# Moving a scan, four left-out steps and the last stores in a TensorE-bound recurrence + MLP kernel

One core of a Trainium2 chip. The metric is the device time of one execution in microseconds; the median of several is given. A "span" is the time from the first to the last instruction in one profiled execution; it is 1.7 to 2.1 us shorter than the time.

## The reference

```python
sig = 1 / (1 + exp(-f_logit))                        # x, f_logit: (4, 6080, 256)
f = lower_bound + (1 - lower_bound) * sig
for t in range(S):                                   # recurrence along the sequence
    h = f[:, t] * h + (1 - f[:, t]) * x[:, t];  y[:, t] = h
h = y.reshape(24320, 256) @ w_in                     # w_in: (256, 2048)
out = (h * cos(h)) @ w_out                           # w_out: (2048, 256), float32 out
```

## The kernel before

The 24,320 tokens are cut into 7 chunks of 256 and 44 of 512. For each chunk ScalarE and GpSimd make the gate `ih` and the input term `u`, the DMA transposes them to `it` and `ut` (for chunks 0 to 3 TensorE does), GpSimd makes the forget factor `ff`, VectorE scans, GpSimd casts the result to `yb`. Then TensorE multiplies by `w_in` (mm1), ScalarE takes the cosine, VectorE the product T, and TensorE multiplies T by `w_out` (moe2). Steps are written (chunk, group). In the traces each engine's instructions come in the program's order (VectorE's scan, T, scan, T of the changed kernel start at 34.60, 35.48, 36.60 and 37.26).

```python
HALVED = (NSMALL, NSMALL + 1, NSMALL + 2)     # NSMALL = 7: 512-token chunks done as two 256s
pa[c, g] = ppool.tile([P, 2 * CH // n, n], f32, tag="p1", bufs=3, ...)   # mm1's output, 3 buffers
# ... cut
def moe2(c, h):
    # ... cut: half of a 128-token tile, 8 matmuls
    if last:
        nc.vector.tensor_copy(osb[:, ts, :], ps[:, ts % 2, :])
        nc.sync.dma_start(out[t0 + ts * P:t0 + (ts + 1) * P, :], osb[:, ts, :])
# ... cut: weaving of the next chunks' gates and scans into the steps
    if c == NPE:                                            # NPE = 4, the fifth chunk
        f, slots = (c - 2, 3), ((c - 2, 3), (c - 2, 3))     # where forget and the two scans go
    elif c <= NSMALL:
        f, slots = (c - 2, 0), ((c - 2, 3), (c - 1, 0))
    else:
        f, slots = (c - 1, 0), ((c - 1, 2), (c - 1, 4))
    at(*f, later(forget, c))
    for i, slot in enumerate(slots):
        at(*slot, later(recur, c, i), later(cast, c, i))
    # ... cut
    at(*second, later(less_one, c), later(pool_term, c), later(turn, c))
at(2, 2, later(emit_load, NSMALL))
SKIP = ((NSMALL, 5), (NSMALL + 1, 3), (NSMALL + 2, 1), (NSMALL + 2, 7))
steps = [(c, h) for c in range(1, NC) for h in range(2 * chunks[c][1] // P)]
for s in range(2, NC):
    if s > 2 and s + 5 < NC:
        emit_load(s + 5)
    for g in range(groups(s)):
        moe1(s, g)                                          # mm1, cosine, product
        if (s, g) not in SKIP:
            moe2(*steps.pop(0))
        for what in weave.get((s, g), []):
            what()
for c, h in steps:
    moe2(c, h)
```

A full-size chunk needs all its T before its second half-step; a small or halved one needs half of them. So moe2 must fall four steps further behind while the kernel passes from small to full chunks: that is what the four left-out steps (SKIP) do. They are made up at the end.

Of the kernel before, what the change touches and what calls it, by code (L numbers as in the profile page):

```python
# [17 lines left out]
def kernel(  # L18
        ctx: ExitStack, tc: tile.TileContext, x: bass.AP, f_logit: bass.AP,
        lower_bound: bass.AP, w_in: bass.AP, w_out: bass.AP, out: bass.AP):  # L20
    nc = tc.nc
# [3 lines left out]
    P = 128  # L25
# [9 lines left out]
    NSMALL = 7  # L35
# [6 lines left out]
    t0 = 0  # L42
# [25 lines left out]
    def hold(what, c, shape, dtype, bufs):  # L68
        if (what, c) not in held:
            held[what, c] = wpool.tile(shape, dtype, tag=what, bufs=bufs,  # L70
                                       name=f"{what}{c}")
        return held[what, c]
# [172 lines left out]
    def groups(c):  # L245
        return NJ * chunks[c][1] // (2 * CH)

    HALVED = (NSMALL, NSMALL + 1, NSMALL + 2)

    def room(c, g):  # L250
        if (c, g) not in pa:
            n = HALF if c in HALVED else chunks[c][1]
            pa[c, g] = ppool.tile([P, 2 * CH // n, n], f32, tag="p1", bufs=3,
# [3 lines left out]
    def mm1(c, g, a=0, b=None):  # L257
        n = chunks[c][1]
        first = 0
        if c in HALVED:  # L260
            n = HALF
# [15 lines left out]
    def cosine(c, g):  # L277
        n = HALF if c in HALVED else chunks[c][1]
        cs[c, g] = wpool.tile([P, 2 * CH // n, n], f32, tag="cs", bufs=3, name=f"cs{c}_{g}")
        nc.scalar.activation(cs[c, g], pa[c, g], AFT.Sin, bias=float(_HALF_PI), scale=1.0)  # L280

    def product(c, g):
        n = HALF if c in HALVED else chunks[c][1]
        jg = 2 * CH // n
        T = wpool.tile([P, jg, n], f16, tag="T", bufs=24, name=f"T{c}_{g}")
        nc.vector.tensor_tensor(T, pa[c, g], cs[c, g], AOP.mult)  # L286
        for jq in range(jg):
            if c in HALVED:
                for ts in (g // 4 * 2, g // 4 * 2 + 1):
                    Tt[c, ts, jg * (g % 4) + jq] = T[:, jq, ts % 2 * P:(ts % 2 + 1) * P]  # L290
            else:
                for ts in range(n // P):
                    Tt[c, ts, jg * g + jq] = T[:, jq, ts * P:(ts + 1) * P]

    def moe1(c, g):
        mm1(c, g)
        cosine(c, g)
        product(c, g)
# [3 lines left out]
    def moe2(c, h):  # L302
        t0, n = chunks[c]
        nt = n // P
        ts, half = h // 2, h % 2
        last = c == NC - 1
        if half == 0 and (ts % 2 == 0 or last):
            p2[c] = ppool.tile([P, 2, D], f32, tag="p2", bufs=2, name=f"pb{c}_{ts}")
        osb = hold("osb", c, [P, CH // P, D], f32, 2)
        ps = p2[c]  # L310
        for jt in range(half * NJ // 2, (half + 1) * NJ // 2):
            nc.tensor.matmul(ps[:, ts % 2, :], Tt[c, ts, jt],  # L312
                             wo[:, jt, :], start=(jt == 0), stop=(jt == NJ - 1))
        if half == 0:
            return
        if last:
            nc.vector.tensor_copy(osb[:, ts, :], ps[:, ts % 2, :])  # L317
            nc.sync.dma_start(out[t0 + ts * P:t0 + (ts + 1) * P, :], osb[:, ts, :])
        elif ts % 2 == 1:
            nc.scalar.copy(osb[:, ts - 1:ts + 1, :], ps)  # L320
            if ts == nt - 1:
                nc.sync.dma_start(
                    out[t0:t0 + n, :].rearrange("(k p) d -> p k d", p=P),
                    osb[:, 0:nt, :])
# [73 lines left out]
    moe1(0, 3)  # L398
    moe1(1, 0)
    moe2(0, 0)  # L400
    gate(2)
    term(2)
# [5 lines left out]
    settle(2)  # L408
    product(1, 2)
    moe2(0, 1)  # L410
    moe1(1, 3)
    moe2(0, 2)
    moe2(0, 3)
    gate(3)
# [7 lines left out]
    def at(s, g, *what):  # L422
        weave.setdefault((s, g), []).extend(what)

    def later(f, *args):
        return lambda: f(*args)

    for c in range(3, NC):
        if c < NPE:
            at(c - 1, 1, later(turn, c), later(forget, c), later(gate, c + 2),  # L430
               later(settle, c))
            continue
        if c == NPE:
            f, slots = (c - 2, 3), ((c - 2, 3), (c - 2, 3))
        elif c <= NSMALL:
            f, slots = (c - 2, 0), ((c - 2, 3), (c - 1, 0))
        else:
# [4 lines that stand above are left out]
        first, second = FRONT.get(c, ((c - 3, groups(c - 3) - 1), (c - 2, 0)))  # L442
        if c != NPE + 1:
            at(*first, later(gate, c))
        at(*second, later(less_one, c), later(pool_term, c), later(turn, c))

    at(2, 2, later(emit_load, NSMALL))
    SKIP = ((NSMALL, 5), (NSMALL + 1, 3), (NSMALL + 2, 1), (NSMALL + 2, 7))
    steps = [(c, h) for c in range(1, NC) for h in range(2 * chunks[c][1] // P)]
    for s in range(2, NC):  # L450
        if s > 2 and s + 5 < NC:
            emit_load(s + 5)
        for g in range(groups(s)):
            moe1(s, g)
            if (s, g) not in SKIP:
                moe2(*steps.pop(0))
# [34 lines left out]
```

## Time and profile before

| | before |
|---|---|
| time, median of 3 | 681.11 us (680.96 to 682.25) |
| span of the profiled execution | 679.7 us |
| TensorE / VectorE / ScalarE / GpSimd busy | 99 / 86 / 76 / 46% |
| granted TensorE clock | 1.000 |

In the timeline each line is a run of like instructions: start, length, engine, line, operation, count and, in brackets, the idle time before it and what ended it. For TensorE compare starts, not lengths (eight matmuls from 35.06 are 1.04 long, and the next eight start 0.87 on). The prediction shows the lines that carry the argument.

### The profile page before, as it was taken

Reading aid. Unit: us, or ns where it says so; the run is one execution under the profiler, and the core shown is the slowest. Engines: PE = TensorE matmul, PEld = TensorE weight load, DVE = VectorE, ACT = ScalarE, POOL = GpSimd, SP = SyncE. Lnnn points to the kernel's source line nnn. Section 1 sums busy time; section 2 is a strip of 40 time slices with the busy share of each in tenths; the row PEclk is TensorE's granted clock in tenths of the full one; section 3 lists DMA queues with packets and bytes.
Section 4 is the critical chain, followed back from the end, with each engine's and each line's share of the span. In section 5 each row is a group of like instructions: output and inputs, shape, how many; then the busy total and the mean of one; then the engine's idle time right before and its main releaser. Section 6 shows DMA issues by size and latency. Waiting matters only on the chain.

```text
span 679.7 us, 12405 instructions
## 1 busy us (share of the span) xinstructions
PE 670.9 (99%) x4826; PEld 494.6 (73%) x4826; DVE 583.2 (86%) x507; ACT 518.2 (76%) x587; POOL 315.1 (46%) x442
## 2 busy tenths in 40 slices
PE   7999999999999999999999999999999999999998
PEld 4899987777777777777777777777777777777776
DVE  5898998888888888888888888888888888888884
ACT  6887788777877788777877788777877788777762
POOL 5478454445454445445454445445454445445300
DMA  8799756656667556764776556764686566632301
GB/s 205 198 259 225 201 157 154 169 140 124 160 188 150 124 140 175 167 139 125 159 189 150 124 142 175 158 148 124 163 185 149 124 144 178 162 76 63 94 32 62
DMA packets 173290, 101.99 MB, mean 150 GB/s; under 512 B 99120, under 2 KB 172080, under 8 KB 173232
## 3 DMA queue, kind: packets, MB, share of 16 engines
q1 hardware_dynamic: 171680, 99.11, 59.5%
q0 software_dynamic: 1280, 2.10, 1.7%
q8 instruction: 37, 0.61, 0.4%
q14 instruction: 21, 0.17, 0.1%
q10 hardware_dynamic: 272, 0.00, 0.0%
HBM read 54.00 MB, written 24.90 MB: 116 GB/s over the span
## 4 chain that ended last, share of the span: by engine, by line
PE 88%; DVE 4%; DMA 3%; issue 2%; ACT 1%; POOL 1%; SPq 0%; ACTq 0%; DVEq 0%; POOLq 0%
PE pb L312 45%; PE pa L271 43%; DVE T L286 3%; DVE ya L218 2%; DMA wo<-in_moe_w_out_dram 1%; DMA wir<-in_moe_w_in_dram 1%; ACT cs L280 1%; DMA zt<-in_f_logit_dram 1%; ACT ig L122 0%; SPq L82 0%; POOL wo L106 0%; POOL u L163 0%; ACT ig L150 0%; POOL xt L82 0%; POOL zt L82 0%
## 5 line engine op out<-in xcount | busy, mean ns | idle before, releaser
L286 DVE TENSOR_TENSOR T<-pa,cs 128x1024 f16<-128x1024 f32 x380 | 449.1, 1212 | 81.5 <-ACT cs L280 81.1
L280 ACT ACTIVATE cs<-pa 128x1024 f32<-128x1024 f32 x380 | 389.3, 1028 | 144.0 <-PE pa L271 132.4
L312 PE MATMUL pb<-wo,T 128*128 128x256 f16 x3040 | 393.0, 273 | 0.6 <-DMA wo<-in_moe_w_out_dram 0.6
L271 PE MATMUL pa<-yb,wi 128*128 128x512 f16 (+2 forms) x1736 | 390.3, 353 | 2.9 <-DMA wi<-in_moe_w_in_dram 1.4
L312 PEld LDWEIGHTS <-T 128*128 128x128 f16 x3040 | 297.3, 98 | 100.1 <-issue 1.0
L271 PEld LDWEIGHTS <-wi 128*128 128x128 f16 x1736 | 193.3, 114 | 75.5 <-issue 2.0
L232 POOL TENSOR_SCALAR yb<-ya,hc 128x512 f16<-128x512 f32 (+1 forms) x97 | 65.8, 679 | 187.5 <-DVE ya L218 186.6
L218 DVE TENSOR_TENSOR_SCAN ya<-ff,ya,ut 128x512 f32<-128x512 f32 (+4 forms) x94 | 131.3, 1398 | 0.6 <-POOL ff L199 0.6
L163 POOL TENSOR_TENSOR u<-ig,xt 128x256 f16<-128x256 f32 x182 | 130.3, 748 | 0.0
L161 POOL CAST ih<-ig 128x1024 f16<-128x1024 f32 (+1 forms) x47 | 47.5, 1010 | 137.1 <-ACT ig L150 135.1
L199 POOL TENSOR_SCALAR ff<-it,hp 128x512 f32<-128x512 f16 (+1 forms) x94 | 62.9, 683 | 1.5 <-DMA it<-ih 1.5
L320 ACT COPY osb<-pb 128x512 f32<-128x512 f32 x93 | 53.8, 579 | 0.7 <-PE pb L312 0.7
L122 ACT ACTIVATE ig<-zt 128x1024 f32<-128x1024 f32 (+2 forms) x52 | 51.7, 994 | 2.0 <-DMA zt<-in_f_logit_dram 1.9
L150 ACT ACTIVATE ig<-ig 128x1024 f32<-128x1024 f32 x44 | 46.9, 1066 | 0.0
L339 PE MATMUL warm<-junk 128*128 128x512 f16 x15 | 5.7, 543 | 1.3 <-POOL junk L328 1.3
L218 DVE TENSOR_TENSOR_SCAN ya<-ff,ya,tp 128x256 f32<-128x256 f32 (+1 forms) x8 | 5.0, 665 | 1.3 <-ACT ff L196 1.3
L218 DVE TENSOR_TENSOR_SCAN ya<-ff,ut 128x320 f32<-128x320 f32 (+2 forms) x6 | 5.6, 928 | 0.0
L317 DVE COPY osb<-pb 128x256 f32<-128x256 f32 x4 | 1.7, 424 | 4.5 <-PE pb L312 4.5
L139 DVE SCALAR_TENSOR_TENSOR u<-ig,xt 128x512 f16<-128x512 f32 (+1 forms) x5 | 3.2, 645 | 2.5 <-DMA xt<-in_x_dram 1.7
L339 PEld LDWEIGHTS <-junk 128*128 128x128 f16 x18 | 2.1, 126 | 4.0 <-issue 2.2
L137 POOL TENSOR_SCALAR ih<-ig 128x512 f16<-128x512 f32 x2 | 1.7, 866 | 6.2 <-ACT ig L122 6.2
L99 POOL CAST wi<-wir 128x512 f16<-128x512 f32 x2 | 1.5, 748 | 4.9 <-DMA wir<-in_moe_w_in_dram 4.8
(29 smaller groups left out, 27.2 us busy)
## 6 DMA issues: line engine op xcount, KB each, us to landing
zt<-in_f_logit_dram SPq DMA_DIRECT2D x44, 512.0 KB, 5.1
xt<-in_x_dram SPq DMA_DIRECT2D x44, 512.0 KB, 6.0
out_dram<-osb SPq DMA_DIRECT2D x43, 512.0 KB, 3.4
out_dram<-osb SPq DMA_DIRECT2D x7, 256.0 KB, 5.1
zt<-in_f_logit_dram SPq DMA_DIRECT2D x5, 256.0 KB, 5.2
xt<-in_x_dram SPq DMA_DIRECT2D x5, 256.0 KB, 5.6
wir<-in_moe_w_in_dram SPq DMA_DIRECT2D x2, 512.0 KB, 5.4
wo<-in_moe_w_out_dram POOLq DMA_DIRECT2D x4, 256.0 KB, 7.1
```

Source lines behind the costliest of these rows:

```text
L122: nc.scalar.activation(ig[:, ks, :], zt[:, ks, :], AFT.Tanh, bias=0.0, scale=0.5)
L150: nc.scalar.activation(ig[:, ks, :], ig[:, ks, :], AFT.Identity, bias=-1.0, scale=1.0)
L161: nc.gpsimd.tensor_copy(by_half(ih), split(ig))
L163: nc.gpsimd.tensor_tensor(by_half(u)[:, k], split(ig)[:, k], split(xt)[:, k], AOP.mult)
L199: nc.gpsimd.tensor_scalar(f[:, a:b], igt[:, i, 0:b - a], hp[:, i:i + 1], 1.0, AOP.mult, AOP.add)
L218: nc.vector.tensor_tensor_scan(ya[:, p:q], f[:, p:q], ut[:, i, p - a:q - a], init, AOP.mult, AOP.add)
L232: nc.gpsimd.tensor_scalar(yb[:, a:b], held[f"ya{i}", c][:, a:b], hc[:, i:i + 1], 0.0, AOP.mult, AOP.add)
L271: nc.tensor.matmul(pa[c, g][:, jq, a:b], win_block(i, jt), held[f"yb{i}", c][:, first + a:first + b], start=(i == 0), stop=(i == ND - 1))
L280: nc.scalar.activation(cs[c, g], pa[c, g], AFT.Sin, bias=float(_HALF_PI), scale=1.0)
L286: nc.vector.tensor_tensor(T, pa[c, g], cs[c, g], AOP.mult)
L312: nc.tensor.matmul(ps[:, ts % 2, :], Tt[c, ts, jt], wo[:, jt, :], start=(jt == 0), stop=(jt == NJ - 1))
L320: nc.scalar.copy(osb[:, ts - 1:ts + 1, :], ps)
```

## The change

The intent: put the fifth chunk's second scan behind a product, so that TensorE gets its buffer back in time; place the left-out steps where VectorE has no scan; and let two engines share the last copies and stores.

```diff
-    HALVED = (NSMALL, NSMALL + 1, NSMALL + 2)
+    HALVED = tuple(range(NSMALL, NSMALL + 4))
...
         if last:
-            nc.vector.tensor_copy(osb[:, ts, :], ps[:, ts % 2, :])
-            nc.sync.dma_start(out[t0 + ts * P:t0 + (ts + 1) * P, :], osb[:, ts, :])
+            for i, (copy, queue) in enumerate(((nc.vector.tensor_copy, nc.sync),
+                                               (nc.scalar.copy, nc.scalar))):
+                ds = slice(i * P, (i + 1) * P)
+                copy(osb[:, ts, ds], ps[:, ts % 2, ds])
+                queue.dma_start(out[t0 + ts * P:t0 + (ts + 1) * P, ds], osb[:, ts, ds])
...
         if c == NPE:
-            f, slots = (c - 2, 3), ((c - 2, 3), (c - 2, 3))
+            f, slots = (c - 2, 3), ((c - 2, 3), (c - 1, 0))
...
-    SKIP = ((NSMALL, 5), (NSMALL + 1, 3), (NSMALL + 2, 1), (NSMALL + 2, 7))
+    SKIP = tuple((c, 6) for c in HALVED)
```

Part 1 is the scans, part 2 the halved chunks with their left-out steps, part 3 the end.

## The prediction

> **What bounds the kernel now.** I read the page first (busy shares), then the groups with shapes kept apart, then the timeline of TensorE, and only where TensorE waits those of VectorE, GpSimd and ScalarE. The groups' columns are: count | busy us, mean ns | idle before.
>
> ```profile
> PE 670.9 (99%) x4826; PEld 494.6 (73%) x4826; DVE 583.2 (86%) x507; ACT 518.2 (76%) x587; POOL 315.1 (46%) x442
> ...
> L286 DVE TENSOR_TENSOR T<-pa,cs 128x1024 f16<-128x1024 f32 x380 | 449.1, 1212 | 81.5 <-ACT cs L280 81.1
> L312 PE MATMUL pb<-wo,T 128*128 128x256 f16 x3040 | 393.0, 273 | 0.6 <-DMA wo<-in_moe_w_out_dram 0.6
> ```
>
> TensorE is 99% busy, but 273 ns is the length of a pipelined matmul, not its pace. The pace is the distance of starts in its timeline:
>
> ```profile
> 35.06 1.04 PE L271 MATMUL pa<-yb,wi 128*128 128x256 f16 x8
> 35.94 1.04 PE L312 MATMUL pb<-wo,T 128*128 128x256 f16 x8
> 37.45 1.03 PE L271 MATMUL pa<-yb,wi 128*128 128x256 f16 x8 [0.47 <-DVE T L286]
> 38.32 1.04 PE L312 MATMUL pb<-wo,T 128*128 128x256 f16 x8
> ...
> 60.15 1.23 PE L271 MATMUL pa<-yb,wi 128*128 128x256 f16 x8
> 61.22 1.04 PE L312 MATMUL pb<-wo,T 128*128 128x256 f16 x8
> ...
> 82.18 1.04 PE L312 MATMUL pb<-wo,T 128*128 128x256 f16 x8
> 83.22 1.03 PE L271 MATMUL pa<-yb,wi 128*128 128x256 f16 x8
> ...
> 98.06 1.04 PE L271 MATMUL pa<-yb,wi 128*128 128x256 f16 x8
> 99.45 1.05 PE L271 MATMUL pa<-yb,wi 128*128 128x512 f16 x4 [0.35 <-DVE T L286]
> ```
>
> Eight 256-column matmuls take 0.873 us from start to start (35.06 to 35.94). One step is a first-product group (L271) plus half a second-product tile (L312), 1.745 us. From 21.5 to 668 us every start follows at this pace except four: 37.45 should be 36.81 (0.64 late), the group of 60.15 stretches by 0.20, 83.22 should be 83.05 (0.17), 99.45 should be 98.93 (0.52). So 1.53 us, 0.2% of the span, is all that any reordering between 21.5 and 668 us can win. After 99.45 all is even.
>
> [...]0.873/8 = 109.1 ns, and four of 512 columns take about 0.864 us. Halving a chunk thus costs some 8 ns a group.
> [...]the four u products (L163) take 2.80 us clear of scans and 4.66 across two scans (54.40 below).
> [...]
> [...]Here the last 128 KB stores land a median of 1.7 us after issue[...].
>
> **Part 1, the fifth chunk's scans in two slots.** The gap at 37.45 waits for a PSUM buffer of three: T of step (3,0) stands on VectorE behind both scans of chunk 4, which themselves waited for GpSimd.
>
> ```profile
> 34.67 1.60 DVE L218 TENSOR_TENSOR_SCAN ya<-ff,ya,ut 128x256 f32<-128x256 f32 x2 [0.61 <-POOL ff L199]
> 36.20 4.61 DVE L286 TENSOR_TENSOR T<-pa,cs 128x1024 f16<-128x1024 f32 x4
> ```
>
> The program order of the changed kernel is scan, T(3,0), scan, T(3,1). Scan 34.67 to 35.5, T to about 36.65, scan to 37.35, T(3,1) to 38.5. The buffer is free at 36.65, before 36.81; the next is wanted at 38.55, so 0.05 to spare. The gap goes: 0.64 us won there. But is it kept? The second scan is 0.85 later, and so are all GpSimd's items behind its cast, down to the transpose (it) for chunk 6, issued at 39.23 now and about 40.1 then. That costs nothing: loads issued from 35.49 fill the queue, and in the packet records the transpose's 256-byte packets start only at 43.6. GpSimd then runs without a pause until TensorE's next stall:
>
> ```profile
> 45.73 0.94 POOL L199 TENSOR_SCALAR ff<-it,hp 128x256 f32<-128x256 f16 x2 [1.27 <-DMA it<-ih]
> 46.62 1.04 POOL L161 CAST ih<-ig 128x1024 f16<-128x1024 f32 x1
> 47.62 3.58 POOL L163 TENSOR_TENSOR u<-ig,xt 128x256 f16<-128x256 f32 x4
> ...
> 54.40 4.66 POOL L163 TENSOR_TENSOR u<-ig,xt 128x256 f16<-128x256 f32 x4
> 59.04 1.36 POOL L232 TENSOR_SCALAR yb<-ya,hc 128x512 f16<-128x512 f32 x2
> ```
>
> The second yb of chunk 7 is done at 60.40; TensorE's group of 60.15 ran two matmuls and waited for it. With part 1 TensorE comes to it at 59.51 but finds the chain started by the same landing (45.7) and of the same length (14.67 us). The group goes on at 60.4 as before. **Part 1 nets 0.0**, at most 0.1 if the scans, now earlier, overlap less with u.
>
> **Part 2, four halved chunks, skips at step 6 of each.** Before, four second-product steps were left out at (7,5), (8,3), (9,1), (9,7); now at (7,6), (8,6), (9,6), (10,6). The work is the same (four left out, done at the end); the halved chunk 10 costs 8 groups x 8 ns = 0.07 us. A step with a skip takes TensorE 0.873 us where VectorE's T alone takes 1.21, so it spends the lead of the buffers; scans stand in steps 2 and 4. From 60.4 on, by hand:
> (7,7) and (8,0) fall at 71.7 and 73.44 as now. (8,6) moves to 83.92, and T(8,3), ending at 83.18, no longer holds it: 0.17 won. (9,0) comes at 86.54, T(8,5) ends about 86.56 plus 0.04 for the semaphore: 0.06 lost anew. (10,0) comes at 99.68, T(9,5) ends about 99.65: 0.01 lost. With (10,0) at 99.69 and one skip of 0.873 still to come, this equals 98.82 against 99.45 now, plus 0.07 for the halving: **part 2 wins 0.56 us**. (11,0) comes at 112.8, T(10,5) about 112.7: no new loss, if barely. The second product keeps its operands: its tightest step now is (7,5), at 69.95, whose T(7,3) ends 69.85 and is used only by its second half.
>
> **Part 3, the last tiles in halves.** The end now (count, then duration ns min/median/max):
>
> ```profile
> 676.43 0.42 DVE L317 COPY osb<-pb 128x256 f32<-128x256 f32 x1 [1.32 <-PE pb L312]
> ...
> L318 SPq DMA_DIRECT2D out_dram<-osb x4: 332/338/345, 671.6 to 676.9; - x4
> ```
>
> Copy to 676.86, store issued 676.89, landed 678.58, span end 679.68. The intent is two copies side by side. But in the built program's order with waits, each of ScalarE's last four copies waits for VectorE, not TensorE: [...]they run one after the other. VectorE's half: 424 ns less 128 columns at 1.04 ns = 0.29, to 676.72. ScalarE's half: 579 ns at 512 columns less 384 at 0.83 = 0.26, plus 0.03 for the wait, to 677.03. The last store is issued at 677.06 instead of 676.89: 0.17 later. Half the bytes save perhaps 0.1. Then the final SyncE sequence checks eight queue semaphores one by one, 0.06 us each: the last landing is now the sixth, with three behind it (678.60 to 678.78); in the changed program it is the first, with seven behind, 0.25 later. **Part 3 loses about 0.3 us.**
>
> Sum: 0.0 - 0.56 + 0.3 = -0.25. From 681.11 that is 680.9.
>
> **Rivals.**
> (a) Part 1's 0.64 survives, because the chain on GpSimd starts earlier or is shorter. For: u takes 4.66 against 2.80, so 1.9 us is contention that moves with the scans. Against: the packets' queue and the unbroken chain. It would make 680.2 to 680.3.
> (b) A new wait: the 0.05 and 0.03 us of room at (4,0), (9,0), (10,0) and (11,0) are as small as my reading errors. If each step-6 skip stalls by 0.2 to 0.4 on T of step 5, part 2 wins nothing: 681.4 to 682.
> (c) The end is helped after all: a 64 KB store lands much faster, as two issues side by side. For: less data per queue.[...] It would make 680.5.
> (d) VectorE becomes the bound. Against: per full chunk it has 8 x 1.21 + 2 x 1.49 = 12.7 us of work in 13.9, and 13.1 in a chunk with a skip, still above.
>
> **Range and chances.** All the winnable stalls and the end together are under 2 us of 681, so 2% (13.6 us) is out of reach both ways. (a) and (c) together reach 679.9; (b) with the end's loss reaches 682. The spread of the three runs before is 1.3 us, upward. So 679.8 to 682.0. Faster by over 2% 0.01, within 2% 0.98, slower 0.01.
>
> **What would show it.** Right: no gap near 37; the first group of chunk 7 broken, resuming at 60.3 to 60.5 after yb; no stall over 0.1 us from 62 to 115; the first full-size group of chunk 11 near 112.8; ScalarE's last copy starting after VectorE's ends; from the last matmul to the span's end about 3.6 us instead of 3.3. Wrong: chunk 7 starting near 59.6 (rival a), stalls on T behind step 6 (b), an end shorter than 3.3 us (c).

## The result

The changed kernel takes 681.80 us (median of 6, 681.31 to 682.95), the kernel before 681.26 on the same occasions (6 runs). The ratio is 1.0009, with a 95% interval of 0.9996 to 1.0022: the same, and no gain to be seen. Ratios here are the mean of one kernel's fast runs over that of the other's of the same rounds, so not quite the ratio of the medians. The profiled span went from 679.7 to 679.9.

First the chain that ended last, by engine, from the page of the kernel before and then of the changed one.

```profile
PE 88%; DVE 4%; DMA 3%; issue 2%; ACT 1%; POOL 1%; SPq 0%; ACTq 0%; DVEq 0%; POOLq 0%
```

```profile
PE 91%; DMA 4%; POOL 3%; issue 1%; DVE 1%; SPq 0%; ACT 0%; POOLq 0%; DVEq 0%
```

VectorE's share of that chain went from 4 to 1% and GpSimd's from 1 to 3: it now runs through GpSimd where it ran through VectorE. (The shares count the work on the chain, not the waits.) TensorE's timeline of the changed kernel shows what it waits for:

```profile
35.90 1.04 PE L312 MATMUL pb<-wo,T 128*128 128x256 f16 x8
36.77 1.04 PE L271 MATMUL pa<-yb,wi 128*128 128x256 f16 x8
...
58.65 1.04 PE L312 MATMUL pb<-wo,T 128*128 128x256 f16 x8
60.17 0.27 PE L271 MATMUL pa<-yb,wi 128*128 128x256 f16 x1 [0.48 <-POOL yb L232]
60.84 0.93 PE L271 MATMUL pa<-yb,wi 128*128 128x256 f16 x7 [0.40 <-POOL yb L232]
...
86.05 1.04 PE L312 MATMUL pb<-wo,T 128*128 128x256 f16 x8
87.07 1.06 PE L271 MATMUL pa<-yb,wi 128*128 128x256 f16 x8
...
113.30 1.03 PE L271 MATMUL pa<-yb,wi 128*128 128x512 f16 x4
```

The gap near 37 is gone. In its place chunk 7's first group waits for both its `yb`: due at 59.53 (58.65 + 0.873), it starts at 60.17 (0.64 late) and is held again after one matmul, which at the pace of 0.109 a matmul costs 0.56 more. The rest of that group goes on at 60.84; in the kernel before it went on at 60.46. Near 83 and 99 nothing is lost any more; near 87 there is a new 0.15.

GpSimd's timeline, changed kernel:

```profile
37.50 0.48 POOL L232 TENSOR_SCALAR yb<-ya,hc 128x256 f16<-128x256 f32 x1 [1.30 <-DVE ya L218]
...
46.16 0.94 POOL L199 TENSOR_SCALAR ff<-it,hp 128x256 f32<-128x256 f16 x2 [1.97 <-DMA it<-ih]
...
54.81 4.63 POOL L163 TENSOR_TENSOR u<-ig,xt 128x256 f16<-128x256 f32 x4
59.43 1.35 POOL L232 TENSOR_SCALAR yb<-ya,hc 128x512 f16<-128x512 f32 x2
```

The chain from the landing of `it` to the second `yb` is as long as before (46.16 to 60.78: 14.62 us; before 14.67). It starts 0.43 later. The transpose itself, from the SyncE queue's timeline, first before, then after:

```profile
39.23 1.29 SPq L184 DMA_TRANSPOSE it<-ih  x1
```

```profile
40.18 1.20 SPq L184 DMA_TRANSPOSE it<-ih  x1
```

It is issued 0.95 later, because GpSimd makes `yb` of the second scan first: the edit puts that scan behind T of step (3,0), and this `yb` stands ahead of chunk 6's gate on GpSimd. The end of the changed kernel:

```profile
676.37 0.29 DVE L320 COPY osb<-pb 128x128 f32<-128x128 f32 x1 [1.46 <-PE pb L312]
676.69 0.27 ACT L320 COPY osb<-pb 128x128 f32<-128x128 f32 x1 [1.48 <-DVE osb L320]
676.99 0.34 ACTq L321 DMA_DIRECT2D out_dram<-osb  x1
```

The two halves stand one behind the other: ScalarE sits idle for 1.48 us and starts 0.03 after VectorE's copy ends. The bracket names VectorE; why the program has that wait was not shown. From the start of the last matmul to the end of the span it is now 3.83 us (before 3.56).

### The profile page after: what moved, and what is told of

Read it like the earlier page. It is cut to its first block, busy times and chain, and to the rows that moved or that the text cites. A ratio compares the mean times of both kernels' runs of the same rounds, so it can differ in the third digit from the quotient of the medians.

```text
span 679.9 us, 12481 instructions
## 1 busy us (share of the span) xinstructions
PE 670.6 (99%) x4858; PEld 497.8 (73%) x4858; DVE 581.7 (86%) x507; ACT 519.6 (76%) x591; POOL 314.3 (46%) x442
## 4 chain that ended last, share of the span: by engine, by line
PE 91%; DMA 4%; POOL 3%; issue 1%; DVE 1%; SPq 0%; ACT 0%; POOLq 0%; DVEq 0%
PE pb L312 46%; PE pa L271 45%; DMA wo<-in_moe_w_out_dram 1%; POOL u L163 1%; DMA it<-ih 1%; DMA wir<-in_moe_w_in_dram 1%; DMA zt<-in_f_logit_dram 1%; POOL ff L199 1%; POOL ih L161 0%; POOL yb L232 0%; SPq L82 0%; DVE ya L218 0%; POOL wo L106 0%; DVE T L286 0%; POOL ig L147 0%
## 5 line engine op out<-in xcount | busy, mean ns | idle before, releaser
L271 PEld LDWEIGHTS <-wi 128*128 128x128 f16 x1768 | 196.6, 114 | 74.7 <-DMA wi<-in_moe_w_in_dram 2.4
```

The lines of the kernel that those rows point to most:

```text
L271: nc.tensor.matmul(pa[c, g][:, jq, a:b], win_block(i, jt), held[f"yb{i}", c][:, first + a:first + b], start=(i == 0), stop=(i == ND - 1))
```

## The experiments

**Why traces and not times decide here.** All kernels have the same instructions up to step (2,2), yet in the profiled executions that step starts anywhere between 27.5 and 29.2 us. That start-up spread is larger than any term in question, and the 95% intervals of the times are about ±0.13%, or ±0.9 us. So I count from the start of step (2,2)'s first group (28.07 in the kernel before) and add up three terms: its start, the body (from there to the start of the last matmul) and the end (from there to the span's end). "Chain" is the start of GpSimd's two `ff` of chunk 6, "second yb" the end of the cast that chunk 7 waits for, both from that mark. Body, end and stalls are read from the records of the single matmuls: a stall is what lies between two starts beyond the pace. Each kernel has one trace. A dash stands for nothing above 0.05. The ratios are to the kernel before in the same rounds, whose medians were 681.16 (e1 to e4), 681.15 (e5 to e8) and 680.99 (e9, e10); e9 and e10 ran on another chip than e1 to e8.

| kernel | step (2,2) | `it` issued | chain | second yb | stalls near 9 / 32 / 55 to 59 / 71 | body | end | time, ratio to before (interval) |
|---|---|---|---|---|---|---|---|---|
| before | 28.07 | 11.15 | 17.66 | 32.33 | 0.64 / 0.19 / 0.17 / 0.51 | 648.05 | 3.56 | 681.26 (with the changed kernel) |
| changed | 28.04 | 12.14 | 18.11 | 32.74 | - / 1.20 / 0.15 / - | 648.01 | 3.83 | 681.80, 1.0009 (0.9996 to 1.0022) |
| e1_scans | 28.20 | 11.92 | 18.15 | 32.79 | - / 1.20 / 0.16 / 0.50 | 648.50 | 3.54 | 682.18, 1.0011 (0.9999 to 1.0024) |
| e2_skips | 27.77 | 10.80 | 17.47 | 32.12 | 0.30 / 0.32 / 0.15 / - | 647.39 | 3.55 | 680.49, 0.9990 (0.9977 to 1.0002) |
| e3_ends | 27.79 | 11.22 | 17.85 | 32.50 | 0.72 / 0.29 / 0.16 / 0.50 | 648.20 | 3.83 | 681.84, 1.0006 (0.9994 to 1.0019) |
| e4_forget_first | 27.50 | 10.95 | 17.36 | 32.08 | - / 0.56 / 0.15 / - | 647.35 | 3.83 | 680.46, 0.9994 (0.9980 to 1.0007) |
| e5_late_xt | 27.51 | 12.19 | 16.94 | 33.09 | - / 1.53 / 0.15 / - | 648.37 | 3.84 | 682.69, 1.0026 (1.0014 to 1.0039) |
| e6_last_half | 28.60 | 12.11 | 18.61 | 33.23 | - / 1.20 / 0.14 / - | 648.50 | 3.52 | 681.58, 1.0004 (0.9992 to 1.0017) |
| e7_three | 29.17 | 10.95 | 15.83 | 32.51 | - / 1.02 / 0.15 / - | 647.79 | 3.54 | 681.22, 1.0000 (0.9986 to 1.0013) |
| e8_scalar_end | 28.40 | 11.39 | 16.26 | 32.73 | 0.08 / 1.07 / 0.15 / - | 648.01 | 3.54 | 681.11, 1.0003 (0.9989 to 1.0017) |
| e9_loads_late | 29.21 | 10.97 | 15.88 | 31.09 | - / - / 0.06 / - | 646.78 | 3.54 | 680.56, 0.9992 (0.9980 to 1.0005) |
| e10_no_split | 27.70 | 11.13 | 16.35 | 31.56 | 0.63 / - / 0.14 / - | 647.39 | 3.56 | 680.42, 0.9990 (0.9976 to 1.0004) |

### Each part alone: e1, e2, e3

e1 is the kernel before with part 1's line alone, e2 with part 2's two lines alone, e3 with part 3's lines alone; their diffs are the three pieces of the diff above.

> Kernel before with part 1 alone (fifth chunk's scans in two slots). Theory A (part 1 moves the wait: it delays GpSimd's items and with them the transpose of chunk 6, so chunk 7's second yb and TensorE's first group of chunk 7 come later): no gap near 37, that group resumes at about 60.8 instead of 60.46, the two gaps near 83 and 99 (0.17 and 0.52) come again about 0.4 later, last matmul about 0.37 later than before (676.5), time about 0.4 us more, ratio about 1.0005. Theory B (the later start in the run after the change was chance of that one execution): the group resumes at 60.4 to 60.5 and the last matmul is at 676.1, time as before.

Theory A held. The group resumed 32.84 after step (2,2), and the body grew by 0.45. The chain starts at 18.15, as in the changed kernel (18.11), against 17.66 before. It wasn't chance: the three executions without part 1 in the old order of loads (before, e2, e3) lie between 17.47 and 17.85, the three with it (changed, e1 and, below, e6) between 18.11 and 18.61. But the spread within each three is 0.4 to 0.5, so the size, 0.45, is known only roughly. TensorE at chunk 7 in e1:

```profile
60.38 0.27 PE L271 MATMUL pa<-yb,wi 128*128 128x256 f16 x1 [0.48 <-POOL yb L232]
61.05 0.93 PE L271 MATMUL pa<-yb,wi 128*128 128x256 f16 x7 [0.40 <-POOL yb L232]
```

> Kernel before with part 2 alone (four chunks in halves, one step left out at step 6 of each). Both theories: gap of 0.64 near 37.4 and the stretch of 0.19 at 60.4 as before; the gaps of 0.17 near 83 and 0.52 near 99 gone, about 0.15 new near 87; halving costs 0.07. Last matmul at about 675.7, 0.4 us earlier than before, time about 680.85, ratio about 0.9994. If the win of part 2 needed part 1's delay, the gaps near 83 or 99 would stay.

The gaps near 83 and 99 went, and 0.15 came back near 87. The body fell by 0.66; of that 0.21 lies in the stalls near 9 and 32 (0.83 together before, 0.62 here), where the two kernels don't differ. So part 2 wins about 0.45: the stalls after chunk 7 fall from 0.70 to 0.18, and the halving takes some 0.07 of that back. The changed kernel against e1 has nearly the same front and says the same: 648.50 to 648.01 is 0.49, of which about 0.05 are small stalls of e1 near 25 and 30.

> Kernel before with part 3 alone (last tiles in halves). Theory: last matmul at 676.12 as before; from its start to the span's end 3.83 instead of 3.56 us: 0.17 from the second copy standing behind the first, less 0.14 that the smaller store is quicker, plus 0.25 from seven instead of three semaphore checks behind the last landing. Time about 0.27 us more. Rival (end is hidden or noise): 3.56.

Exactly as expected: the end takes 3.83 in place of 3.56.

### Part 1 without the delay: e4

```diff
@@ changed kernel
-        at(*f, later(forget, c))
+        if c != NPE + 1:
+            at(*f, later(forget, c))
         for i, slot in enumerate(slots):
+            if (c, i) == (NPE, 1):
+                at(*slot, later(forget, c + 1))      # chunk 5's ff ahead of chunk 4's second scan and cast
             at(*slot, later(recur, c, i), later(cast, c, i))
```

> Changed kernel with chunk 5's two gate items on GpSimd put ahead of chunk 4's second scan and cast, so that GpSimd isn't delayed by part 1: transpose of chunk 6 issued at about 39.3 to 39.5 instead of 40.18. Theory A (the issue time carries through to the landing): lands at about 45.65 instead of 46.07, first group of chunk 7 resumes at about 60.4 instead of 60.84, last matmul about 675.65, time 0.4 us under the changed kernel. Theory C (the queue of loads alone sets the landing, and 0.4 was chance or comes from elsewhere): landing no earlier, group resumes at 60.8, last matmul about 676.06.

`it` is issued at 10.95 again, the chain starts at 17.36, the stall falls from 1.20 to 0.56, and the body by 0.66 against the changed kernel. So the issue time carries through to the landing, and the order on GpSimd is what cost part 1 its loss. The same two lines in e4, the first without a wait:

```profile
58.96 0.27 PE L271 MATMUL pa<-yb,wi 128*128 128x256 f16 x1
59.63 0.93 PE L271 MATMUL pa<-yb,wi 128*128 128x256 f16 x7 [0.40 <-POOL yb L232]
```

But the body equals that of e2 (647.35 against 647.39), which has no part 1 at all: with the chain where it was, part 1 is worth nothing. The two chains start at 17.36 and 17.47, and in both TensorE goes on as soon as chunk 7's second `yb` is done (32.08 and 32.12).

### What sets the start of the chain: e5

```diff
@@ changed kernel: the x load of chunk 8 (512 KB) goes behind the transposes of chunk 6
-            emit_load(s + 5)
+            emit_load(s + 5, which=(0,) if s == 3 else (0, 1))
...
+    at(3, 1, lambda: emit_load(NSMALL + 1, which=(1,)))
```

`which` picks the logits (0), x (1) or both; the lines that add it to `emit_load` aren't printed here.

> Changed kernel with one 512 KB load (x of chunk 8) issued behind the two transposes of chunk 6 instead of ahead of them. Times from the start of step (2,2). Theory A (the transpose waits in the queue behind the loads, and its landing sets GpSimd's chain and so the stall at chunk 7's first group): the first 256-byte packets come about 1.4 earlier (14.2 instead of 15.68), GpSimd's chain starts at about 16.7 instead of 18.11, the stalls of 0.64 and 0.56 near 32 shrink to under 0.1 together, last matmul at about 646.9 instead of 648.01, time about 1.1 us under the changed kernel. Rival (the chain's length or the scans set the stall, not its start): the stall stays at over 0.8.

Half of it came true. The first 256-byte packets of the transposes came 1.4 earlier (14.30), and the chain started 1.17 earlier (16.94). But the stall grew to 1.53. GpSimd's timeline of e5 shows the next link:

```profile
44.45 0.94 POOL L199 TENSOR_SCALAR ff<-it,hp 128x256 f32<-128x256 f16 x2 [0.67 <-DMA it<-ih]
...
52.32 1.36 POOL L199 TENSOR_SCALAR ff<-it,hp 128x512 f32<-128x512 f16 x2 [1.51 <-DMA it<-ih]
```

The `ff` of chunk 7 now waits 1.51 us for its own transpose, which stands in the queue (issued at 46.39) behind the moved load, a store and both loads of chunk 9 (issued from 42.71 to 44.40). The chain that I had read as unbroken has a second gate; as long as the first was later, it was hidden. The times of e5 are also worse (1.0026) than its trace, whose span is 679.7; what the untraced executions did differently stays open.

### The end, apart: e6 and e8

e6 is the changed kernel with halves in the last tile alone.

```diff
         if last:
+            if ts < nt - 1:                          # three whole tiles, as before
+                nc.vector.tensor_copy(osb[:, ts, :], ps[:, ts % 2, :])
+                nc.sync.dma_start(out[t0 + ts * P:t0 + (ts + 1) * P, :], osb[:, ts, :])
+                return
```

> Changed kernel with the halves in the last tile alone (three whole tiles by VectorE, as before). Theory: the last store stands at another of the eight queue semaphores, two checks behind it instead of seven, so 5 x 0.062 = 0.31 less: from the last matmul to the end 3.52 instead of 3.83, with the copies still one behind the other (last store issued 0.93 after the last matmul, as in the changed kernel). Rival (the end is long for the second queue or the smaller stores): 3.8. Body as in the changed kernel, 648.0.

3.52, as expected, with the last store issued 0.93 after the last matmul, as late as in the changed kernel. Three stores fewer move the last one to another queue semaphore, and the final row of checks behind it is shorter. (The body, 648.50, has 0.5 of stalls more between 24 and 30 than the changed kernel's; I did not pursue that.)

e8 is e7 (next) with the last tile copied whole by ScalarE and stored from its queue.

> As the kernel with three parts of its own and the old end, but the last tile is copied whole by ScalarE and stored from its queue. A 256-column copy there should take 579 - 256 x 0.83 = 0.37 us against VectorE's 0.42, and the last store keeps its place among the semaphores, so from the last matmul to the end about 3.50 instead of 3.56. If the other queue costs more: 3.6 or over.

The copy took 0.37 and the store was issued 0.71 after the last matmul instead of 0.76, but it landed 2.44 after it, like e7's (2.44). The end stays 3.54: the 0.05 is lost between issue and landing (1.73 against 1.69 us).

### Both gates moved: e7 and e9

e7 joins parts 1 and 2, e4's order, e5's late load and the old end. e9 adds this:

```diff
             if s > 2 and s + 5 < NC:
-                emit_load(s + 5, which=(0,) if s == 3 else (0, 1))
+                if s != 4:
+                    emit_load(s + 5, which=(0,) if s == 3 else (0, 1))
...
     at(3, 1, lambda: emit_load(NSMALL + 1, which=(1,)))
+    at(4, 0, later(emit_load, NSMALL + 2))           # chunk 9's loads behind chunk 7's transposes
```

> Parts 1 and 2, chunk 5's gates first, x of chunk 8 behind the transposes, and the end of the kernel before. Theory A: no stall near 9 and none over 0.1 near 32; only some 0.15 near 58; from step (2,2) to the last matmul 646.7 to 646.9 (648.05 before), end 3.56: about 1.2 us under the kernel before, ratio 0.998. If chunk 8's later load makes a new wait for GpSimd or ScalarE, it shows as a stall between 20 and 60.

Missed, for the reason e5 found: the chain starts at 15.83, GpSimd then idles 1.44 for the transpose of chunk 7, and the stall is 1.02.

> As the kernel with three parts of its own (e7), and both 512 KB loads of chunk 9 behind the two transposes of chunk 7 too. Theory A, sharpened after e5 and e7 (GpSimd's chain to chunk 7's yb has two gates, the landings of the transposes of chunk 6 and of chunk 7, both queued behind loads): GpSimd no longer idles 1.4 us ahead of chunk 7's gate items (L199); chunk 7's second yb ends by 31.0 after step (2,2) instead of 32.51; the stalls of 0.46 and 0.56 near 32 fall under 0.1 together; from step (2,2) to the last matmul 646.8 instead of 647.79. Rival (the landings aren't set by the loads in front): GpSimd idles as long, stall 1.0. A new wait may come for chunk 9's own gate or chunk 8's transposes, between 32 and 40.

As expected, to 0.02 us: body 646.78. GpSimd and then TensorE in e9:

```profile
45.09 0.94 POOL L199 TENSOR_SCALAR ff<-it,hp 128x256 f32<-128x256 f16 x2
...
52.02 1.36 POOL L199 TENSOR_SCALAR ff<-it,hp 128x512 f32<-128x512 f16 x2
```

```profile
59.77 1.04 PE L312 MATMUL pb<-wo,T 128*128 128x256 f16 x8
60.65 1.04 PE L271 MATMUL pa<-yb,wi 128*128 128x256 f16 x8
61.52 0.71 PE L312 MATMUL pb<-wo,T 128*128 128x256 f16 x5
```

Neither `ff` waits, and chunk 7's first group (60.65) comes in pace. From step (2,2) on TensorE loses 0.18 until the last chunk's first late product: 0.09 near 45 and 0.09 near 58 (each a stall of 0.06 and one of 0.03). That product comes 0.14 late in every kernel here.

### Part 1 with the chain early: e10

e10 is e9 without part 1: the slots are `((c - 2, 3), (c - 2, 3))` again, and chunk 5's `ff` where they were.

> The same late loads and part 2, but without part 1 (both scans of the fifth chunk in one slot, chunk 5's gates in their old place). If part 1 is worth its gap once GpSimd's chain is early: a gap of 0.3 to 0.7 near 9 comes back and nothing near 32 takes it up, so from step (2,2) to the last matmul 0.3 to 0.7 more than e9. If part 1 is worth nothing even then: equal to e9.

A gap of 0.63 is back, and nothing further on takes it up:

```profile
35.56 1.04 PE L312 MATMUL pb<-wo,T 128*128 128x256 f16 x8
37.06 1.03 PE L271 MATMUL pa<-yb,wi 128*128 128x256 f16 x8 [0.46 <-DVE T L286]
```

The body is 647.39, 0.61 more than e9's. So part 1 is worth its whole gap once chunk 7's `yb` isn't what TensorE meets next.

e9's body and end together are 1.29 us (0.2%) under the kernel before. The stalls account for it: 1.68 from step (2,2) on before, 0.32 in e9, less 0.07 for the halving; so it isn't a matter of the other chip. The times don't resolve it: 0.9992, interval 0.9980 to 1.0005. It beats both kernels by these two terms alone; its whole span, 679.5, is only 0.2 shorter than before, because its step (2,2) started 1.14 later.

## Why the prediction was right or wrong

The range (679.8 to 682.0) and the class held. That was hardly a test of the mechanism, since by the prediction's own count under 2 us were at stake. The point, 680.9, was 0.9 under the measured 681.8, and the sign of the small change came out the other way: 0.25 less was expected, the medians say 0.54 more, and the spans 0.2 more. In the traces the miss lies in part 1 (0.45) and part 2 (0.1); what the medians add to it is within the noise. Of the signs named, the gap near 37 went, ScalarE's last copy came after VectorE's, and the end grew by 0.27 as said. Chunk 7's first group went on at 60.84 and not by 60.5, there was a stall of 0.15 near 87, and chunk 11 began at 113.30 instead of 112.8.

**What bounds the kernel: right.** TensorE's four late starts were all that could be won between 21.5 and 668 us; e9, which removes them, wins 1.27 of the 1.53 in the body, having taken on the 0.07 of the halving (estimated) and 0.18 of small new stalls.

**Part 1: the gap was read rightly, one step failed.** The gap near 37 went, and chunk 7's first group took the gain. The failed step is "That costs nothing: loads issued from 35.49 fill the queue", and with it "the chain started by the same landing (45.7)". The packets do start at the same time (43.60 before, 43.72 after), but the landing is 0.43 later when the issue is 0.95 later. e1 shows 0.45 lost where I had 0.0, e4 that an earlier issue brings it back. The records of the single DMA packets in the traces show where the time goes. The two transposes are 1,024 packets of 256 bytes. Before, the last starts at 45.39, and `it` lands 0.24 after it ends. In the changed kernel 97% have started by 45.04, earlier than before (45.27), but the last 25 follow one by one, some 0.03 us apart, until 45.83, and `it` lands 0.22 after that. Such a tail stands in the four traces where `it` is issued 11.92 or more after step (2,2) (changed, e1, e5, e6), and in none of the eight where it is issued by 11.39. So the first packet's start didn't fix the landing. Why the last packets trail stays open. Two readings were off without consequence: the second scan comes 1.04 later (35.56 to 36.60), not 0.85, and the group of 60.15 had run one matmul, not two, when it waited.

**Part 2: right, and a little smaller.** 0.56 expected, about 0.45 measured: 0.66 from before to e2 with 0.21 of front-end chance in it. The new loss stood at (9,0), where I put 0.06; it was 0.15, and 0.03 more in the same group. TensorE started 0.05 to 0.06 after the end of the T that released it (37.45, 83.22 and 99.45 before, 87.07 after), where I had 0.04. The 0.07 of the halving is an estimate, eight times the prediction's 8 ns; over the steady part of the trace the groups take 0.873 and 0.863, 10 ns apart, which would make it 0.08.

**Part 3: right, term by term.** The last store is issued 0.93 after the last matmul instead of 0.76 (0.17, as worked out); the store of half the bytes takes 1.55 instead of 1.70 from issue to landing (0.14, said perhaps 0.1); from the landing to the span's end it takes 1.35 instead of 1.10, 0.25 more, with the checks 0.062 apart as before. By column the copies cost 1.03 ns on VectorE (424 ns at 256, 292 at 128) and 0.82 on ScalarE (579 at 512, 266 at 128), where I had 1.04 and 0.83. Sum 0.27, said 0.3. (Before, the last store's semaphore was the fifth of the eight, not the sixth; that three stand behind it is right.)

**The rivals.** (a) did not come true in the changed kernel, but e9 and e10 make it true by moving loads. The scans do show in the u products: in the kernel before, the two of 54.40's four that start inside a scan take 1.65 and 1.67 us, the two that start ahead of one 0.74. (In the groups of 2.80, as at 368.16, a scan begins only during the last product.) (b) came as 0.15 in one place, far from enough to undo part 2. (c) is out: the store is quicker by 0.14, less than what the copies' order and the checks cost. (d) never showed: after chunk 9's first group no stall is over 0.02 until the last chunk in the changed kernel.

## What to carry to other kernels

Before removing a stall on a saturated engine, look up the next thing that engine will meet, and ask what that thing hangs on; a removed stall is only won if everything behind it is early too (part 1's gap was worth nothing in e4 against e2, 647.35 and 647.39, and 0.61 in e9 against e10), and here that was a GpSimd chain fed by transposes queued behind loads that nobody needed yet. When an operation is moved, follow what stands behind it in order on the engine that consumes it: the 0.95 us by which GpSimd held back the transpose cost more than the scan's place on VectorE won (e1: 0.45 lost on balance). A chain read as unbroken may hold a second gate that the first one hides (1.51 us in e5). And the start of a transfer's first packet doesn't say when it lands: here the first packets came at 43.60 and 43.72, the landings were 0.43 apart, and they came 0.24 and 0.22 after the last packet ended.

## What else the traces show

- Eight matmuls of 256 columns take TensorE 0.873 us from start to start and four of 512 columns 0.863, 216 ns each, in every step of the steady part (120 to 660 us, both kernels).
- The last store of 128 KB took 1.70 us from issue to landing (SyncE, kernel before; 1.73 from ScalarE's queue in e8), the last two of 64 KB 1.55 (SyncE and ScalarE, changed kernel). A straight line through 1.70 and 1.55 would leave about 1.40 us at no bytes, an estimate from these two sizes alone.
- VectorE's last copies took 291 to 293 ns at 128 columns and 424 at 256; ScalarE's copies 266 at 128, 372 at 256 (e8) and 579 at 512.
- At the program's end SyncE checks the eight semaphores by which DMAs report their landing one by one, about 0.062 us each (678.60, 678.66, 678.72 and 678.78 for the last four in the kernel before), so which of them the last store uses is worth up to 0.4 us (estimated, 7 x 0.062); three stores fewer (e6) shortened the end by 0.31.
- In the changed kernel the last packets of two transposes trailed: 25 of 1,024, over some 0.8 us (to 45.83).
